# Loading gates late, reordering weights and gathers, and ranking the third batch after the loop, in a fused mLSTM and mixture-of-depths kernel

## The chip, the cores and the metric

The kernel runs on one core of one Trainium2 chip. The metric is device time in microseconds (us) for one execution; lower is better. The core has a matrix engine (PE, with its weight loads shown apart as PEld), a vector engine (DVE), a scalar engine (ACT), a general engine (POOL) and a queue engine (SP) which here only issues transfers. Each engine works through its own instructions strictly in the order of the program; engines wait for each other and for transfers on semaphores.

## The reference

```python
# mLSTM cell: q, k, v, o_gate (4, 8, 768, 40), i_gate, f_gate (4, 8, 768)
for t in range(S):
    m_new = np.maximum(f_gate[:, :, t] + m, i_gate[:, :, t])
    f_stab = np.exp(f_gate[:, :, t] + m - m_new)
    i_stab = np.exp(i_gate[:, :, t] - m_new)
    m = m_new
    C = f_stab * C + i_stab * outer(vt, kt)            # per head, 40 x 40
    n = f_stab * n + i_stab * kt
    h_tilde = C @ qt
    denom = np.maximum(np.abs(n @ qt), 1.0)
    y[:, :, t] = sigmoid(o_gate[:, :, t]) * h_tilde / denom
x = y.transpose(0, 2, 1, 3).reshape(4, 768, 320)
# mixture of depths, capacity 128 of 768 tokens per batch
scores = x @ w_gate
out = x.copy()
for b in range(4):
    top_idx = argpartition(-scores[b], capacity)[:capacity]
    xe = x[b, top_idx]
    ye = np.maximum(xe @ w1, 0) @ w2                   # 320 -> 1024 -> 320
    out[b, top_idx] = xe + sigmoid(scores[b, top_idx])[:, None] * ye
```

## The kernel before, in words

All data is float32. The sequence of each batch is cut into three pieces of 256 tokens, so there are N = 12 steps, three per batch; step n belongs to batch n // 3. The schedule is written out by hand: every call in the loop `for n in range(N)` issues its instructions to the engines at that place, and nothing reorders them.

One step of the recurrence consists of these calls, with their lines in the profile. `scores(n)` (L307) multiplies keys and queries on PE into `pS`; `masked(n)` (L313) applies the causal mask on DVE. `turn(n + 1, "kT")` (L241, copies by ACT at L243) transposes the next keys, `widen(n + 1)` (L225, ACT) spreads the next queries. `update(n + 1)` (L274) makes the next state updates in `pU` from keys and the weighted values `wv`; `states(n + 1)` (L286 to L294) sums them on DVE. `read(n)` (L329) multiplies the queries with the state, `turn(n + 1, "qT")` (L241, copies L245) transposes the next queries, `attend(n)` (L339) adds the part inside the piece, and `divide(n)` (L348 to L353) makes `y` on DVE. `weigh(n)` (L253, POOL) forms `wv` from the loaded values.

A second group of calls turns `y` into output rows: `sigmoid(n)` (L257, ACT) on the loaded gate `o`, `output(n)` (L361, POOL) into the row tile `x`, `router(n)` (L376, DVE) for the scores, `store(n)` (L368, SP) to memory. There are four gate buffers, three buffers each of k, q and v, two row tiles `x` (batches alternate), and four buffers of `y`.

The third group is the mixture of depths for a whole batch. `spread(b, ...)` (L404 PE, L408 ACT) copies the scores of a batch to all partitions; `ranks(b)` counts for each token how many scores are larger, three columns on DVE (`greater`, L414) and three on ACT (`signs`, L419); `select(b)` (L453) makes a selection matrix, `numbers(b)` (L498) turns it into row numbers on PE, `fetch(b)` (L504) gathers the 128 chosen rows from memory by POOL's queue. `fetched(b)` (L514) transposes them, `valued(b)` (L524) computes their gates, `layer1` (L543, L547) and `layer2` (L559) are the two matrix products, `weighed(b)` (L564) scales and `add(b)` (L568) adds the rows to the output with a scattering transfer. The last batch is ranked in two parts (`ranks_first`, `ranks_last`) and its rows are picked by matrix products (`picked`, L479) and not by a gather.

SP issues all loads and stores in one queue: `load(n)` (two transfers each for v and k, one for q), `load_o(n)` (L75, four transfers), `store(n)` (two). `load(n + 3)` stands at the head of step n and carries the gate of step n + 2 with it until step 5; the weights of both layers are issued at the head of step 5 behind step 8's loads. The gates of steps 6 to 8 come with `load(9)`.

In the order before, batch 0 is spread at the end of step 3, ranked in step 5 and its layers stand in step 8; batch 1 is spread at the end of step 6, ranked in step 7, and its layers stand in steps 9 and 10; batch 2 is spread at the end of step 9, ranked and gathered in step 10, and its layers stand in and behind step 11. `fill` calls issue matrix products without use.

## Time and profile before

| | |
|---|---|
| time, median of 4 runs | 168.75 us (167.16 to 170.33) |
| the profiled execution's own time | 169.06 us |
| its span in the profile | 167.3 us |
| granted clock of TensorE, mean | 0.984 |
| PE busy | 147.9 us (88%) |
| PEld, DVE, ACT, POOL busy | 128.1, 95.9, 76.0, 68.3 us |
| transferred | 24.14 MB, mean 144 GB/s |
| read and written in memory | 19.04 MB, 4.59 MB |

The span is what the profile's records cover; 1.76 us of the execution's own time lie around it. PE's busy time counts every matrix product from start to modelled end, so 88% does not mean that the array is used to 88%. The transfers are made of rows of 160 bytes for k, v and o, and of 320 bytes for q; of 94,424 packets 88,465 are smaller than 512 bytes. Start times of instructions below are from the start of the span.

### The profile page before, as it was taken

The page shows a single profiled execution, that of the slowest core. Times are in us where ns is not written, and L with a number is a line of the kernel's source. Part 1 is how long each engine was busy: PE and PEld are TensorE (multiplying, and loading weights), DVE is VectorE, ACT ScalarE, POOL GpSimd, SP SyncE. Part 2 cuts the span into 40 slices and gives each one's busy share as a digit, 9 for nine tenths or more (in the row PEclk, how much of TensorE's full clock was granted, in tenths as well). Part 3 has the DMA queues.
Part 4 walks back from the last instruction along what each step waited for, and adds up shares of the span by engine and source line. Part 5 has one row for each costly group of instructions (what it writes and reads, how often), then busy time and mean ns, then how long its engine had stood idle before and what let it go on. Part 6 is the DMA issues. An engine that isn't in the chain of part 4 may idle for free.

```text
span 167.3 us, 6707 instructions
## 1 busy us (share of the span) xinstructions
PE 147.9 (88%) x2872; PEld 128.1 (77%) x2872; DVE 95.9 (57%) x250; ACT 76.0 (45%) x144; POOL 68.3 (41%) x89
## 2 busy tenths in 40 slices
PE   7979999799989699797999988859999999999930
PEld 7769989697969599696897777639869989799710
DVE  6477466376646998769630039845695796802000
ACT  1567564443645852394321353423934339521110
POOL 7036393928092808162006028942520682230030
PEclk9999999999999999999999999978999999999997
DMA  4999989898898889689969986999778261330003
GB/s 90 195 162 157 155 164 155 160 158 163 139 196 144 152 141 250 114 197 309 318 157 205 214 161 101 171 179 173 136 158 232 62 104 22 80 35 4 8 12 43
DMA packets 94424, 24.14 MB, mean 144 GB/s; under 512 B 88465, under 2 KB 93778, under 8 KB 94386
## 3 DMA queue, kind: packets, MB, share of 16 engines
q1 hardware_dynamic: 93472, 22.36, 70.1%
q0 software_dynamic: 720, 1.15, 4.0%
q8 instruction: 24, 0.39, 1.0%
q10 hardware_dynamic: 194, 0.13, 0.3%
q14 instruction: 14, 0.11, 0.2%
HBM read 19.04 MB, written 4.59 MB: 141 GB/s over the span
## 4 chain that ended last, share of the span: by engine, by line
PE 30%; DMA 30%; SPq 18%; POOL 8%; issue 5%; DVE 3%; ACT 2%; POOLq 1%; ACTq 0%; DVEq 0%
DMA v<-in_v_dram 13%; SPq L64 8%; DMA k<-in_k_dram 7%; SPq L75 6%; POOL wv L253 6%; PE py L559 5%; PE pU L543 5%; PE pt L241 4%; DMA q<-in_q_dram 4%; DMA w<-in_moe_w_dram 4%; PE pU L274 4%; PE pH L339 3%; SPq L68 3%; DMA o<-in_o_gate_dram 2%; PE pH L329 2%
## 5 line engine op out<-in xcount | busy, mean ns | idle before, releaser
L253 POOL TENSOR_TENSOR wv<-v,cols 64x656 f32<-64x656 f32 x23 | 30.6, 1333 | 51.9 <-DMA v<-in_v_dram 43.0
L361 POOL TENSOR_TENSOR x<-y,o 128x320 f32<-128x320 f32 x24 | 21.2, 919 | 10.0 <-DVE x L394 3.8
L243 ACT COPY kT<-pt 128x512 f32<-128x512 f32 x24 | 13.6, 586 | 18.8 <-PE pt L241 18.6
L245 ACT COPY qT<-pt 128x512 f32<-128x512 f32 x24 | 13.8, 634 | 17.1 <-PE pt L241 17.1
L241 PE MATMUL pt<-ident,k 128*128 128x128 f32 x96 | 14.8, 284 | 5.7 <-DMA k<-in_k_dram 5.2
L286 DVE TENSOR_TENSOR C<-pU,C 128x164 f32<-128x164 f32 x40 | 13.1, 328 | 10.7 <-PE pU L274 9.6
L376 DVE CUSTOM_DVE_ANT_0 scr<-x,wg 128x320 f32<-128x320 f32 x22 | 16.1, 730 | 3.8 <-POOL x L361 1.8
L559 PE MATMUL py<-w,hT 128*128 128x320 f32 x64 | 18.2, 437 | 0.0
L274 PE MATMUL pU<-wv,k 128*64 128x82 f32 x384 | 17.1, 245 | 0.5 <-POOL wv L253 0.5
L241 PEld LDWEIGHTS pt<-ident,k 128*128 128x128 f32 x96 | 10.9, 144 | 8.6 <-issue 3.5
L274 PEld LDWEIGHTS pU<-wv,k 128*64 128x64 f32 x384 | 15.1, 143 | 2.6 <-POOL wv L253 1.5
L339 PE MATMUL pH<-wv,P 128*64 128x82 f32 x384 | 16.5, 237 | 0.0
L339 PEld LDWEIGHTS pH<-wv,P 128*64 128x64 f32 x384 | 14.5, 136 | 2.0 <-issue 1.5
L559 PEld LDWEIGHTS py<-w,hT 128*128 128x128 f32 x64 | 11.8, 190 | 4.7
L329 PE MATMUL pH<-C,qT 40*64 40x41 f32 x704 | 14.3, 229 | 0.8 <-issue 0.8
L313 DVE TENSOR_TENSOR P<-pS,mask 128x1024 f32<-128x1024 f32 x12 | 14.6, 1215 | 0.6 <-PE pS L307 0.6
L241 PE MATMUL pt<-ident,qw 128*128 128x128 f32 x96 | 13.1, 279 | 1.9 <-ACT qw L225 1.9
L307 PE MATMUL pS<-qT,kT 40*64 40x64 f32 x768 | 14.3, 221 | 0.3 <-ACT qT L245 0.3
L329 PEld LDWEIGHTS pH<-C,qT 40*64 40x64 f32 x704 | 12.7, 134 | 2.3 <-issue 1.1
L307 PEld LDWEIGHTS pS<-qT,kT 40*64 40x64 f32 x768 | 12.5, 134 | 1.7 <-ACT qT L245 0.5
L568 POOL DMA_INDIRECT out_dram<-yg,idx x4 | 6.4, 1603 | 16.8 <-ACT yg L564 16.3
L419 ACT ACTIVATE sgn<-sb,x 128x768 f32<-128x768 f32 (+2 forms) x16 | 12.8, 801 | 0.4
(138 smaller groups left out, 213.6 us busy)
## 6 DMA issues: line engine op xcount, KB each, us to landing
k<-in_k_dram SPq DMA_DIRECT2D x24, 160.0 KB, 4.6
q<-in_q_dram SPq DMA_DIRECT2D x12, 320.0 KB, 5.4
v<-in_v_dram SPq DMA_DIRECT2D x24, 160.0 KB, 4.3
o<-in_o_gate_dram SPq DMA_DIRECT2D x48, 80.0 KB, 3.7
out_dram<-x SPq DMA_DIRECT2D x24, 160.0 KB, 3.6
w<-in_moe_w_dram SPq DMA_DIRECT2D x2, 640.0 KB, 8.9
w<-in_moe_w_dram SPq DMA_DIRECT2D x2, 512.0 KB, 6.4
w1c<-in_moe_w_dram SPq DMA_DIRECT2D x4, 64.0 KB, 5.3
```

What stands on the lines that cost most here:

```text
L241: PE.transpose(pt[:, p, :], src[:, c, 2 * p:2 * p + 2, :].rearrange("s j d -> s (j d)"), ident)
L243: ACT.copy(out=T[:, :, 128 * c:128 * c + 128], in_=pt)
L245: ACT.copy(out=T.rearrange("e p (u t) -> e t p u", t=2)[:, c], in_=pt)
L253: (DVE if n == 0 and r else POOL).tensor_tensor(out=wv_t[n % 3][o, :, :, r], in0=v_t[n % NB][o], op=OP.mult, in1=cols[s][o, 0:2, b * H:b * ...
L274: PE.matmul(pU[64 * j:64 * j + 64, c, p], k_t[n % NB][:, c, 2 * p + j, :], wv_t[n % 3][:, c, 2 * p + j], start=True, stop=True)
L307: PE.matmul(pS[o, j, c, p, :], kT[e, p, t], qT[e, p, t], start=True, stop=True)
L313: DVE.tensor_tensor(out=P.rearrange(flat), in0=pending[n].pop("pS").rearrange(flat), op=OP.mult, in1=mask.unsqueeze(1).to_broadcast([128, ...
L329: PE.matmul(g["pH"][64 * c:64 * c + 64, NP * j + p, r], g["qT"][e, p, t], state[n, 2 * c + r][e, p, :], start=(c, j) not in g["begun"], st ...
L339: PE.matmul(g["pH"][64 * c:64 * c + 64, NP * j + p], g["P"][:, j, c, p, :], wv_t[n % 3][:, c, 2 * p + j], start=(c, j) not in g["begun"], ...
L361: POOL.tensor_tensor(out=x.rearrange(order, j=2, d=D), in0=pending[n]["y"][:, r].rearrange("s (j p) d -> s j p d", j=2), in1=o.rearrange(o ...
L376: DVE.tensor_tensor_reduce(out=scr, in0=x[:, r, 0:DM], in1=wg, scale=1.0, scalar=0.0, op0=OP.mult, op1=OP.add, accum_out=x[:, r, DM:DM + 1])
L559: PE.matmul(d["py"], d["hT"][:, f, :], w2[:, f, :], start=(f == 0), stop=(f == NF - 1))
```

## The change

Gates: `load` no longer carries the gate of step n + 2. The gates of steps 0 to 3 are issued behind the loads of steps 3, 5, 6 and 7, those of steps 4 and 5 behind the loads of step 9, those of steps 6 to 9 at the head of step 9 behind the stores of steps 3 to 5, and those of steps 10 and 11 behind the whole loop. `opened(n)`, that is `sigmoid` and `output`, moves with them: steps 0 to 5 are opened in steps 3, 4, 5, 7, 8, 8 and steps 6 to 10 behind the loop. There are eight buffers of `y`.

Weights: they are issued in step 6 behind step 8's loads and the stores of steps 0 to 2, and ahead of step 9's loads.

Batches: batch 0 is spread and ranked at the end of step 6, selected and gathered in step 7, with its layers in step 8; batch 1 is ranked at the end of step 9, gathered in step 10, with both layers behind the loop. Batch 2 is ranked in two parts, gathered, and computed behind the loop. Useless products stay in two places only.

```diff
     def load(n):
-        if n < N:
-            load_kv(n, v_t, v)
-            load_kv(n, k_t, k)
-            for i in {8: (2,), 9: (3, 4, 5)}.get(n, ()):
-                store(i)
-            load_q(n)
-            for i in {7: (0, 1)}.get(n, ()):
-                store(i)
-        for i in {7: (), 8: (), 9: (6, 7, 8), 11: (), 12: (10, 11)}.get(n, (n - 1,) if n <= N else ()):
+        load_kv(n, v_t, v)
+        load_kv(n, k_t, k)
+        load_q(n)
+        for i in {3: (0,), 5: (1,), 6: (2,), 7: (3,), 9: (4, 5)}.get(n, ()):
             load_o(i)
...
-            (DVE if n == 0 and r else POOL).tensor_tensor(out=wv_t[n % 3][o, :, :, r], in0=v_t[n % NB][o], op=OP.mult,
+            (DVE if n in (0, 10) and r else POOL).tensor_tensor(out=wv_t[n % 3][o, :, :, r], in0=v_t[n % NB][o], op=OP.mult,
...
+    def opened(n):
+        sigmoid(n)
+        output(n)
...
     for n in range(N):
-        if n > 0:
+        if 0 < n < 9 and n != 6:
             load(n + 3)
-        if n == 5:
-            ...                               # the weights
         scores(n)
+        if n == 10:
+            weigh(11)
         masked(n)
+        if n == 6:
+            for i in range(3):
+                store(i)
+            weights()
+            load(9)
...
+        if n in (7, 10):
+            select(n // 3 - 2)
         if n == 8:
+            fetched(0)
+            valued(0)
             layer1(0, 0)
             layer1(0, 4)
-            layer2(0, 0, 4)
-            layer2(0, 4)
-        if n == 10:
-            layer2(1)
-        if given:
-            ranks(b - 1)
-            select(b - 1)
...
+            layer2(0)
+            weighed(0)
+            weigh(9)
+            opened(4)
+        for i in {4: (0,), 5: (1,), 6: (2,), 8: (3,), 9: (4, 5)}.get(n, ()):
+            router(i)
         if n == 9:
-            fetched(1)
-            ...
-            layer1(1, 0)
-            layer1(1, 4)
+            for i in range(3, 6):
+                store(i)
+            for i in range(6, 10):
+                load_o(i)
         if more:
-            turn(n + 1, "kT", (0, 2, 2, 2, 2, 3, 4, 5)[n] if n < 8 else 0)
+            turn(n + 1, "kT", {6: 2, 9: 4}.get(n, 0))
             widen(n + 1)
         if 0 < n and more:
             update(n + 1)
+            if n == 7:
+                numbers(0, spare(8)[:, 1, 0:3])
+                fetch(0)
             states(n + 1)
         read(n)
         if n == 10:
-            numbers(b - 1, spare(n + 1)[:, 1, 0:3])
-        if n + 2 < N and n != 8:
+            numbers(1, spare(11)[:, 1, 0:3])
+            fetch(1)
+        if n < 7:
             weigh(n + 2)
...
             turn(n + 1, "qT")
-            if b > 0 and s == 0:
-                dep[b - 1] = {"sb": spread(b - 1, 0, 2 * NS)}
...
+        if n in (6, 9):
+            i = n // 3 - 2
+            dep[i] = {"sb": spread(i, 0, 2 * NS)}
+            ranks(i)
         attend(n)
         divide(n)
+        for i in {3: (0,), 4: (1,), 5: (2,), 7: (3,), 8: (5,)}.get(n, ()):
+            opened(i)
         if n == 8:
+            weigh(10)
+            add(0)
...
+    opened(6)
+    opened(7)
+    fetched(1)
+    layer1(1, 0)
+    valued(1)
+    opened(8)
+    for i in range(6, 9):
+        router(i)
+        store(i)
+    load_o(10)
+    load_o(11)
+    dep[2] = {"sb4": spread(2, 0, 4, ps_h)}
+    layer1(1, 4)
+    opened(9)
+    sb = spread(2, 4, 6, ps_h)
+    ranks_first(2)
+    ranks_last(2, sb)
+    select(2)
+    layer2(1, 0, 6)
+    numbers(2, ps_t.tile([128, 3], FP, name="pi", tag="t"))
+    layer2(1, 6)
+    router(9)
+    opened(10)
+    fetch(2)
+    weighed(1)
+    router(10)
+    store(9)
+    store(10)
+    sigmoid(N - 1)
+    gated(N - 1)
+    add(1)
     b = B - 1
+    dep[b] = {"sb4": spread(b, 0, 4)}
+    fetched(2, 2)
+    layer1(2, 0)
+    valued(2)
+    ranks_first(b)
     router_last(N - 1)
     output(N - 1)
     layer1(b - 1, 4)
-    ranks_last(b)
+    ranks_last(b, spread(b, 4, 6))
     store(N - 1)
     layer2(b - 1)
     weighed(b - 1)
     picked(b)
     ...                                       # as before
```

## The prediction

> **What bounds the kernel now.** I read the page first (busy shares, chain), then PE's timeline, the windows of ten microseconds, and the waits. The chain of the page and the longest wait say that transfers and PE share the span:
>
> ```profile
> PE 30%; DMA 30%; SPq 18%; POOL 8%; issue 5%; DVE 3%; ACT 2%; POOLq 1%; ACTq 0%; DVEq 0%
> ...
> POOL wv L253 <- DMA v<-in_v_dram: 43.0, 9, 12.0
> ```
>
> DMA and SP's issuing (SPq) make 48% of the chain, and the weighting of values waits 43.0 us for v. That is the loop. PE's timeline (start, duration, instructions) gives the steps, since each begins with the scores L307, and the end:
>
> ```profile
> 20.32 1.50 PE L307 MATMUL pS<-qT,kT 40*64 40x64 f32 x64
> ...
> 62.77 1.16 PE L307 MATMUL pS<-qT,kT 40*64 40x64 f32 x64
> ...
> 72.44 1.16 PE L307 MATMUL pS<-qT,kT 40*64 40x64 f32 x64
> ...
> 81.48 1.16 PE L307 MATMUL pS<-qT,kT 40*64 40x64 f32 x64
> ...
> 100.30 1.16 PE L307 MATMUL pS<-qT,kT 40*64 40x64 f32 x64
> ...
> 118.64 1.16 PE L307 MATMUL pS<-qT,kT 40*64 40x64 f32 x64
> 119.73 4.57 PE L559 MATMUL py<-w,hT 128*128 128x320 f32 x16
> ...
> 130.50 1.20 PE L307 MATMUL pS<-qT,kT 40*64 40x64 f32 x64
> ...
> 146.23 1.50 PE L479 MATMUL pU<-sel_f,x 128*128 128x128 f32 x12
> ```
>
> I write S6 for the start of step 6 and so on: steps 1, 6, 7, 8, 9, 10, 11 start at 20.3, 62.8, 72.4, 81.5, 100.3, 118.6 and 130.5. The windows (length, then busy time of PE, PEld, DVE, ACT, POOL, then granted clock, DMA share, GB/s) show what limits which part:
>
> ```profile
> 40.00:50.00 10.00, 9.45 (x234) 8.27 (x232) 5.75 (x14) 5.48 (x9) 5.23 (x6) 1.00 0.87 152
> ...
> 110.00:120.00 10.00, 8.58 (x195) 7.79 (x196) 4.49 (x13) 5.12 (x10) 3.86 (x3) 0.83 0.95 160
> ...
> 140.00:150.00 10.00, 10.00 (x70) 8.49 (x69) 5.83 (x22) 5.42 (x16) 3.44 (x3) 1.00 0.22 41
> ```
>
> To 120 us the DMA engines are loaded to 0.8 and more; from 130 us they are nearly free and PE never stops: from S11 to the end, 36.8 us, the kernel is PE's own work without a gap.
>
> **The change, part 1: the loop up to S11.** A step's own products, from start to start, are scores 1.1, keys 1.0, update 1.3, read 1.1, queries 1.0, attend 1.3: 6.8 us. Loads of a step are k, q, v 0.98 MB and the gate 0.33 MB, together 1.31 MB; at the 149 to 170 GB/s of the windows from 10 to 60 us (mean 158) that is 8.3 us, and this is what steps 1 to 8 last now. Without the gate it is 6.2 us, less than PE's 6.8. So steps 1 to 5 become PE's: S6 = 20.3 + 5 x 6.8 = 54.3, 8.5 earlier. The useless products removed (0.28 us each) are hidden now by the wait for loads and are not counted as a gain. Step 6 keeps two (0.55) and has the spread (0.8): S7 = 62.4.
>
> Step 7 has a new wait. The ranks now stand in front of `divide(6)` on DVE and the numbers in the middle of step 7 on PE. The spread ends at 61.2; ACT's copy 0.8, three counts of 1.06 and a correction 0.2, `divide` 1.5, mask 1.2, selection 1.0, numbers 0.3 (rows L408, L414, L426, L348 to L353, L313, L453, L498) end at 69.3. PE finished its update at 65.8 and stands 3.2 us; behind the numbers are read, queries and attend, 3.4: S8 = 72.7. The index takes 0.6 and the gather goes out at 70.0; with the median 4.5 us of the table of issues (3.0 to 6.2) it lands at 74.5, after step 8's scores (73.8). Transposes 0.5, copies 0.8, two halves of layer one at 2.7, layer two 4.5: 85.7.
>
> The transfers by then: up to the queries of step 8, nine loads and four gates and the small gates of the start, 10.4 MB at 158 GB/s from 2 us: 67.6. Stores 0 to 2 and weights, 3.6 MB at the 300 GB/s of the page's slices 19 and 20, take 12 us: 79.6, before layer two needs them. Step 9's load 85.8, gate 4 87.9, gate 5 90, step 10's load 96.2, step 11's 102.4. `opened(4)` puts the sigmoid of gate 4 on ACT ahead of the copies of step 9's keys, which are queued behind it, and PE's queries behind those: 87.9 + sigmoid 0.75 + copies 1.1 + queries widened 0.75 + transposes 1.0 + attend 1.3 gives S9 = 92.8. If the gate is early, yg and PE's own work behind the layers set 91.7; at 149 GB/s the gate lands at 92.3 and S9 is 97.2.
>
> Step 9: scores 1.1, four useless products 1.1, keys, update, read, queries 4.4, spread 0.8, attend 1.3 are 8.7; DVE has divide 1.5, the half of `weigh(10)` 1.66 (row L253 of DVE), mask 1.2 and four routers at 0.58 ahead of the spread, 6.7, as late as PE. S10 = 101.6. Step 10 repeats step 7's wait: from the spread, 1.3 before S10, copy 0.8, counts 3.4, divide 1.5, mask 1.2, selection 1.0, numbers 0.3, then queries and attend 2.3: S11 = S10 + 9.2 = 110.8. That is 19.7 us earlier than 130.5. Ten of it are not gained but carried behind the loop: both layers of batch 1 (5.4 and 4.5).
>
> **Part 2: from S11 to the end.** Times from S11. Read waits for `divide(10)` to 1.5; attend ends at 4.1, `fetched(1)` 4.6, copies 5.5, first half of layer one 8.2, its relu on ACT 8.8. Only then come, in ACT's order, the small gate and the sigmoid of step 8 (9.75); output 1.7 on POOL (11.5), the router's second half (12.4), the second spread 0.5 (12.9). Meanwhile ACT has a copy, a relu and the sigmoid of step 9 and ends the copy of the second spread at 13.9. The ranks of batch 2 follow on ACT, with these rows (four of the first, three of 0.51 with the same 0.19, and gaps):
>
> ```profile
> 138.43 0.71 ACT L419 ACTIVATE sgn<-sb,x 128x512 f32<-128x512 f32 x1
> 139.04 0.19 ACT L419 ACTIVATION_READ_ACCUMULATOR sgn<-sb,x 128x1 f32 x1
> ```
>
> that is 4 x 0.85 + 3 x 0.63 = 5.3: 19.2. DVE joins the counts 0.4, selects 1.0, numbers and index 0.9: 21.6. The gather without traffic beside it takes 3.0:
>
> ```profile
> 131.05 1.05 POOL L504 DMA_INDIRECT xe<-out_dram,idx  x1 [8.86 <-DVE den L349]
> ```
>
> (`fetched(2)` ran at 134.09). It lands at 24.7; the spread of batch 3, two useless products and the transposes end at 25.9, copies 26.8, layer one's first half 29.5. PE, which had layer two of batch 1 in between, stands about 4.4 us (16.3 to 20.7) and again some 2. From there on the order is that of before: its relu started at 137.85 and the first half of the last selection was ready some 7.8 us later, so `picked` starts at 37.5, and from it (146.23) to the end are 21.1 as before. Sum 58.6 against 36.8: 21.8 more.
>
> **Part 3: the clock.** The row of 110 to 120 us shows 0.83: PE stood for 1.0 and 1.7 us around 109 to 111, and keys and update then took 1.09 and 2.23 in place of 0.66 and 1.35 us. That is 10 x 0.17 = 1.7 us for one drop. The hole of 4.4 us behind the loop is longer; I count one drop, 1.7. Bounds: none, 0, if layer one comes after the clock is back; three, 5.1, with those of steps 7 and 10. The Trainium skill, TensorE: Matmul & The Clock Gate, section "What's actually happening", says that the clock falls to half after an idle window of about 3.4 us and comes back after one of work. By that rule only the hole behind the loop counts, 172.9 in all; by this trace, where two holes of 2.7 us together were enough, step 7's would count too. The rule speaks against a change that opens a hole of 4.4 us.
>
> **Sum.** 110.8 + 58.6 + 1.7 = 171.1 of span against 167.3, and 1.76 around it: 172.9 us. The profiled execution took 169.06, 0.2% above the median of 168.75.
>
> **Rivals.** (1) Slower transfers: at 149 GB/s gate 4 is 4.4 later and so is all behind it: 177.3. For it: most windows of the loop lie at 149 to 165. Against: without gates there are fewer, larger transfers in the queue. (2) No difference: the gates come at 170 GB/s (S9 = 91.7) and the clock holds: 109.7 + 58.6 + 1.76 = 170.1, within 1%, which is about what a measurement can tell from no change. (3) Faster: the ranks and the gather of batch 2 run beside PE's work, so that behind S11 only that work counts: 36.8 as now, and layers, transposes, spread and numbers carried there, 12.0: 48.8. Then 110.8 + 48.8 + 1.76 = 161.4; if half of the chain is hidden, 166.3. It decides from the point where step 8's router ends by S11 + 4 and not at 12.4, 8 us earlier. For it: POOL and DVE have idle time in steps 10 and 11, and gates 6 to 9 land by about 114 us. Against: step 8's sigmoid stands behind a relu of layer one on ACT, and the routers stand behind `divide(11)` on DVE. (4) That the gates' removal brings nothing because PE stays behind anyway is excluded for steps 1 to 5: the wait for v is 43 us.
>
> **Chances.** Forecast 0.45; slow transfers 0.18; no difference 0.15; faster 0.22. The forecast's own range is 170 (no gate wait, no drop) to 178 (two more drops, a gather of 6.2). The range reaches down to 165.5, past half of the hidden chain, and up to 178. Faster 0.22, same 0.15, slower 0.63.
>
> **What would show it.** Right: S6 near 54, S7 near 62, a stand of PE of 3 us in step 7 ahead of L494 (the numbers), S9 near 93 with ACT waiting for o ahead of the copies of the keys, S11 near 111, a hole on PE ahead of the numbers of batch 2, and `picked` 37 us behind S11. Wrong: S11 well before 108, or no hole behind the loop, would make it faster; S9 at 97 or more points to the transfers.

## The result, and the profile after

The changed kernel takes 186.03 us (median of 12 runs, 183.03 to 191.0); the kernel before takes 169.06 us beside it (17 runs). The ratio is 1.095, 95% interval 1.090 to 1.100. The profiled execution took 183.03 us with a span of 180.9 us, at a mean granted clock of 0.933 (before: 167.3 us, 0.984). Executions of one kernel spread by a few per cent; ratios are formed without the disturbed ones ("none" stands below where too few were left), and the profiled executions of e2_pick2, e8_step9, e9_early_gather and e10_tail2 are disturbed ones, so that their starts are rather too late and their tails too long.

The profile's chain of work that ended last, shares of the span by engine:

```profile
PE 55%; DVE 12%; DMA 10%; issue 7%; SPq 6%; ACT 3%; POOL 3%; POOLq 0%; DVEq 0%; ACTq 0%
```

Transfers and SP's issuing were 48% of it and are now 16%. What takes their place is PE, DVE and "issue". The waits (total, times, longest) say the same of the values:

```profile
POOL wv L247 <- DMA v<-in_v_dram: 29.7, 7, 6.3
```

PE's timeline (start, duration, instructions, in brackets the idle time before) has the starts of the steps, in the order 1, 6, 7, 8, 9, 10, 11 (the rows of L301 without idle time before them), the idle times that no wait explains ("issue"), and the last selection:

```profile
17.55 1.21 PE L268 MATMUL pU<-wv,k 128*64 128x82 f32 x27 [0.79 <-issue]
...
21.00 1.15 PE L301 MATMUL pS<-qT,kT 40*64 40x64 f32 x61
23.13 0.33 PE L301 MATMUL pS<-qT,kT 40*64 40x64 f32 x3 [0.98 <-issue]
...
40.98 0.31 PE L323 MATMUL pH<-C,qT 40*64 40x41 f32 x2 [0.31 <-issue]
...
57.17 0.93 PE L301 MATMUL pS<-qT,kT 40*64 40x64 f32 x48
59.33 0.46 PE L301 MATMUL pS<-qT,kT 40*64 40x64 f32 x16 [1.23 <-issue]
...
66.55 1.16 PE L301 MATMUL pS<-qT,kT 40*64 40x64 f32 x64
...
73.03 0.31 PE L494 MATMUL pU<-place,sel 128*128 128x3 bf16 x6 [1.82 <-DVE sel L449]
73.27 1.14 PE L323 MATMUL pH<-C,qT 40*64 40x41 f32 x64
74.35 1.60 PE L235 MATMUL pt<-ident,qw 128*128 128x128 f32 x8
75.88 2.45 PE L333 MATMUL pH<-wv,P 128*64 128x82 f32 x32
78.26 1.16 PE L301 MATMUL pS<-qT,kT 40*64 40x64 f32 x64
81.21 0.52 PE L510 MATMUL pX<-ident,xe 128*128 128x128 f32 x3 [1.79 <-DMA xe<-out_dram,idx]
82.19 3.38 PE L539 MATMUL pU<-xeT,w 128*128 128x128 f32 x16 [0.46 <-ACT xeT L512]
...
99.63 1.16 PE L301 MATMUL pS<-qT,kT 40*64 40x64 f32 x64
...
109.86 1.16 PE L301 MATMUL pS<-qT,kT 40*64 40x64 f32 x64
...
117.53 0.29 PE L494 MATMUL pU<-place,sel 128*128 128x3 bf16 x6 [1.73 <-DVE C L280]
...
120.67 1.99 PE L301 MATMUL pS<-qT,kT 40*64 40x64 f32 x64
...
140.67 0.32 PE L494 MATMUL pi<-place,sel 128*128 128x3 bf16 x6 [3.93 <-DVE sel L449]
...
147.50 3.17 PE L539 MATMUL pU<-xeT,w 128*128 128x128 f32 x16 [0.46 <-ACT xeT L512]
...
159.21 1.50 PE L475 MATMUL pU<-sel_f,x 128*128 128x128 f32 x12
```

Set beside before and the forecast (us; "tail" is from S11 to the end of the span):

| | S1 | S6 | S7 | S8 | S9 | S10 | S11 | tail | span |
|---|---|---|---|---|---|---|---|---|---|
| before | 20.3 | 62.8 | 72.4 | 81.5 | 100.3 | 118.6 | 130.5 | 36.8 | 167.3 |
| forecast | 20.3 | 54.3 | 62.4 | 72.7 | 92.8 | 101.6 | 110.8 | 60.3 | 171.1 |
| after | 21.0 | 57.2 | 66.6 | 78.3 | 99.6 | 109.9 | 120.7 | 60.2 | 180.9 |

So the late gates do make steps 1 to 6 faster, by 5.9 us at S7. By S9 the lead is 0.7 us: the wait for the gathered rows and 2.45 us for an `attend` that takes 1.36 at full clock stand in the rows above. At S11 the lead is 9.8 us, and that is no more than batch 1's layers (9.9 us), which before stood in steps 9 and 10 and now stand behind the loop. The tail is 23.4 us longer. The windows (length, busy PE, PEld, DVE, ACT, POOL, clock, DMA share, GB/s):

```profile
40.00:50.00 10.00, 9.69 (x276) 8.72 (x272) 7.07 (x17) 6.13 (x10) 5.99 (x6) 1.00 0.93 153
70.00:80.00 10.00, 7.60 (x206) 6.72 (x204) 5.89 (x16) 3.04 (x5) 2.94 (x3) 0.83 0.92 278
...
110.00:120.00 10.00, 6.94 (x208) 6.38 (x207) 7.77 (x20) 5.82 (x13) 0.77 (x1) 0.96 0.66 107
140.00:150.00 10.00, 8.30 (x33) 5.89 (x34) 6.27 (x23) 2.57 (x7) 7.92 (x8) 0.51 0.48 98
```

Before, the window 140 to 150 had PE busy for 10.00 at full clock. Now it follows the hole of 3.93 us and runs at 0.51. On ACT the ranks of batch 2 that the hole waits for:

```profile
136.71 0.72 ACT L416 ACTIVATE sgn<-sb,x 128x512 f32<-128x512 f32 x1
137.33 0.19 ACT L416 ACTIVATION_READ_ACCUMULATOR sgn<-sb,x 128x1 f32 x1
```

### The profile page after: what moved, and what is told of

Its sections match the earlier page's. It is cut to its first block, busy times and chain, and to the rows that moved or that the text cites. A ratio compares the mean times of both kernels' runs of the same rounds, so it can differ in the third digit from the quotient of the medians.

```text
span 180.9 us, 6677 instructions
## 1 busy us (share of the span) xinstructions
PE 151.8 (84%) x2840; PEld 130.3 (72%) x2840; DVE 96.0 (53%) x259; ACT 76.8 (42%) x153; POOL 67.6 (37%) x88
## 4 chain that ended last, share of the span: by engine, by line
PE 55%; DVE 12%; DMA 10%; issue 7%; SPq 6%; ACT 3%; POOL 3%; POOLq 0%; DVEq 0%; ACTq 0%
PE pt L235 9%; PE pH L333 6%; PE pU L268 6%; PE pU L539 6%; DMA xe<-out_dram,idx 5%; PE pS L301 5%; PE py L555 5%; PE pH L323 4%; SPq L75 3%; PE ph L539 3%; PE warm L102 3%; DVE scr L370 3%; DMA v<-in_v_dram 2%; DVE P L307 2%; DVE cmp L411 2%
## 5 line engine op out<-in xcount | busy, mean ns | idle before, releaser
L247 POOL TENSOR_TENSOR wv<-v,cols 64x656 f32<-64x656 f32 x22 | 29.4, 1338 | 40.8 <-DMA v<-in_v_dram 29.7
L555 PE MATMUL py<-w,hT 128*128 128x320 f32 x64 | 19.5, 457 | 0.0
L333 PE MATMUL pH<-wv,P 128*64 128x82 f32 x384 | 18.5, 252 | 0.4 <-DVE P L307 0.4
L333 PEld LDWEIGHTS pH<-wv,P 128*64 128x64 f32 x384 | 16.1, 148 | 2.7 <-issue 1.6
L301 PE MATMUL pS<-qT,kT 40*64 40x64 f32 x768 | 15.5, 229 | 2.6 <-issue 2.2
L370 DVE CUSTOM_DVE_ANT_0 scr<-x,wg 128x320 f32<-128x320 f32 x22 | 14.6, 664 | 3.7 <-POOL x L355 1.4
L301 PEld LDWEIGHTS pS<-qT,kT 40*64 40x64 f32 x768 | 13.5, 142 | 4.3 <-issue 2.8
L416 ACT ACTIVATE sgn<-sb,x 128x512 f32<-128x512 f32 (+2 forms) x20 | 14.4, 722 | 0.6
L235 PE MATMUL pt<-ident,k 128*128 128x128 f32 x96 | 13.4, 279 | 1.2 <-DMA k<-in_k_dram 1.0
L539 PE MATMUL pU<-xeT,w 128*128 128x128 f32 x80 | 12.6, 323 | 2.1 <-ACT xeT L512 1.4
L539 PEld LDWEIGHTS pU<-xeT,w 128*128 128x128 f32 x80 | 11.8, 234 | 3.3 <-ACT xeT L512 2.4
```

What stands on the lines that cost most here:

```text
L235: PE.transpose(pt[:, p, :], src[:, c, 2 * p:2 * p + 2, :].rearrange("s j d -> s (j d)"), ident)
L247: (DVE if n in (0, 10) and r else POOL).tensor_tensor(out=wv_t[n % 3][o, :, :, r], in0=v_t[n % NB][o], op=OP.mult, in1=cols[s][o, 0:2, b * ...
L301: PE.matmul(pS[o, j, c, p, :], kT[e, p, t], qT[e, p, t], start=True, stop=True)
L333: PE.matmul(g["pH"][64 * c:64 * c + 64, NP * j + p], g["P"][:, j, c, p, :], wv_t[n % 3][:, c, 2 * p + j], start=(c, j) not in g["begun"], ...
L370: DVE.tensor_tensor_reduce(out=scr, in0=x[:, r, 0:DM], in1=wg, scale=1.0, scalar=0.0, op0=OP.mult, op1=OP.add, accum_out=x[:, r, DM:DM + 1])
L416: ACT.activation(out=sgn[:, 0:w], in_=sb, func=AF.Sign, bias=own, scale=-1.0, accum_out=cnt)
```

## The experiments

The first theory after the result: the tail is as forecast; the miss lies in the loop, S11 9.9 us later than forecast, through PE's holes, the chain of batch 0 in steps 6 to 8 and the counts of batch 1 in steps 9 and 10. The rival was that half clock explains most of it. All starts are from the profiled executions:

| kernel | S7 | S8 | S9 | S11 | tail | clock | median us | ratio to before, 95% |
|---|---|---|---|---|---|---|---|---|
| after | 66.6 | 78.3 | 99.6 | 120.7 | 60.2 | 0.933 | 186.0 | 1.095 (1.090 to 1.100) |
| e1_fill | 65.3 | 75.4 | 99.6 | 119.4 | 59.6 | 0.992 | 180.8 | 1.079 (1.062 to 1.097) |
| e2_pick2 | 67.9 | 78.1 | 102.7 | 124.5 | 56.7 | 0.932 | 182.8 | none |
| e3_pick01 | 65.5 | 73.3 | 99.4 | 116.2 | 60.5 | 0.953 | 181.3 | 1.086 (1.073 to 1.098) |
| e4_gates_early | 71.5 | 83.4 | 105.8 | 127.7 | 57.5 | 0.926 | 189.1 | 1.130 (1.112 to 1.149) |
| e5_tail | 65.7 | 77.8 | 99.5 | 125.4 | 57.5 | 0.901 | 186.4 | 1.108 (1.101 to 1.115) |
| e6_nogate | 64.7 | 76.4 | 96.5 | 118.4 | 59.9 | 0.933 | 180.1 | 1.068 (1.059 to 1.076) |
| e7_pick_pool | 65.3 | 75.7 | 99.9 | 116.7 | 61.8 | 0.933 | 179.9 | 1.063 (1.054 to 1.072) |
| e8_step9 | 65.9 | 77.7 | 100.5 | 121.8 | 60.9 | 0.926 | 185.1 | none |
| e9_early_gather | 68.4 | 86.6 | 104.5 | 122.0 | 60.3 | 0.925 | 181.8 | 1.067 (1.053 to 1.082) |
| e10_tail2 | 68.8 | 81.7 | 102.9 | 125.3 | 59.3 | 0.898 | 182.4 | 1.078 (1.067 to 1.089) |
| e11_gather2 | 69.9 | 76.7 | 94.6 | 111.4 | 60.8 | 0.962 | 176.8 | 1.044 (1.032 to 1.056) |
| e12_tail_fill | 66.9 | 77.0 | 100.4 | 120.5 | 56.4 | 0.976 | 177.8 | 1.065 (1.049 to 1.080) |
| e13_both | 77.1 | 83.9 | 104.0 | 124.1 | 56.1 | 0.948 | 182.2 | 1.080 (1.073 to 1.088) |
| e14_chain0 | 76.8 | 83.6 | 103.0 | 124.2 | 61.4 | 0.911 | 187.1 | 1.109 (1.100 to 1.117) |

**e1_fill: useless products in PE's holes.**

```diff
+ fill(..., 6)          # step 7, ahead of numbers(0); 7 ahead of the gathered rows of batch 0
+ fill(..., 5), (..., 6)  # step 10, ahead of read and of numbers(1); 14 and 3 more in the tail
```

> The changed kernel with useless matrix products put into the places where PE stands: 6 ahead of the numbers of batch 0 in step 7, 7 ahead of the transposes of the rows of batch 0 in step 8, 5 ahead of read(10) and 6 ahead of the numbers of batch 1, 14 ahead of the numbers of batch 2, and 5 in place of 2 ahead of the transposes of the rows of batch 2. Theory of the exposed chain (behind the start of step 11 PE waits for the ranks and the gather of batch 2, 13.5 us more than the work carried there): PE waits for the same things, only the slow products behind the holes get their clock back, which is at most 1.7 us each for step 7, step 8, step 10 and the hole behind the loop; 2 to 5 us less than the change, 178 to 182 us, mean clock above 0.96. Rival, the clock (mean 0.933 against 0.984, 9 us of full-speed work over the span): 8 to 9 us less, 175 us. If the products themselves are in the way: no change or slower.

The clock rose to 0.992, but the span fell only from 180.9 to 179.0 us, and S9 did not move. The half clock alone is therefore not the miss: the time, 180.8 us, is the theory's, and the rival's 175 lies below the interval. PE then waited longer for what it had waited for before: 2.77 us instead of 1.79 for the gathered rows of batch 0.

**e2_pick2: counts of batch 2 replaced by a fixed table.**

```diff
- ranks_first(2); ranks_last(2, sb)
+ dep[2]["cnt"] = perm      # numbers and gather ahead of layer2(1)
```

> The changed kernel without the ranking of batch 2: its counts are left out, a fixed table in their place picks 128 rows, and selection, numbers and gather stand right behind the second spread and ahead of layer two of batch 1; the spreads stay. Theory of the exposed chain: the gather of batch 2 goes out as soon as the stores of steps 6 to 8 have landed, at about 136 us in place of 142.3, and layer one of batch 2 starts some 6 us earlier, with a smaller hole on PE; 6 to 9 us less than the change, 175 to 178 us. Rival, the clock: what falls away is only the hole, 2 to 3 us. Rival, late gates: no gain beyond the step 9 routers, under 2 us.

In this trace the tail fell by 3.5 us, against the theory's 6 to 9. The hole ahead of the numbers went from 3.93 to 0.55 us, but a stand of 2.52 us ahead of batch 3's spread came up, for routers whose gates, 10 and 11, are issued only behind store 8. The chain of batch 2 is real, and another wait of nearly its length lies behind it.

**e3_pick01: counts of batches 0 and 1 replaced by the table.**

```diff
- ranks(i)
+ dep[i]["cnt"] = perm
```

> The changed kernel without the counts of batches 0 and 1 (the spreads stay); a fixed table picks their rows. Theory: the counts stand ahead of divide(6) and divide(9) on DVE and hold PE in steps 7 and 10; without them step 8 starts 3 us earlier and the gather of batch 0 goes out as soon as the stores of steps 0 to 2 have landed (75 us, as now), so that step 9 starts at most 1 to 2 us earlier; step 11 starts 2 us earlier against step 10; together 3 to 5 us less than the change, 179 to 181 us. Rival, transfers set step 9: nothing from step 7, 2 us from step 10 at most. Rival, the counts are the main loss of the loop: 8 us or more less.

S7 to S8 fell from 11.7 to 7.8 us and S9 to S11 from 21.0 to 16.8: those are the prices of the counts. But S9 stayed, as the theory had it. PE's timeline of this kernel:

```profile
73.34 1.16 PE L303 MATMUL pS<-qT,kT 40*64 40x64 f32 x64
81.22 0.87 PE L512 MATMUL pX<-ident,xe 128*128 128x128 f32 x3 [6.72 <-DMA xe<-out_dram,idx]
```

The index was ready by 70.6 us, POOL issued the gather at 74.25, and PE stood 6.72 us instead of 1.79.

**e4_gates_early: gates 0 to 5 loaded where they were before (six gate buffers), all else as changed.**

```diff
- 3: (0,), 5: (1,), 6: (2,), 7: (3,), 9: (4, 5)
+ 1: (0,), 3: (2,), 4: (3,), 5: (4,), 6: (5,)    # and gate 1 behind load_q(2)
```

> The changed kernel with the gates of steps 0 to 5 loaded where the kernel before loads them (behind the loads of steps 1 to 6, six gate buffers), and opened where the change opens them. Theory of the exposed chain: steps 1 to 6 go back to 8.5 us each, step 7 starts at about 72, but the transfers ahead of step 9 are the same bytes in all, so that the loss at step 9 is 2 to 5 us; behind the loop nothing changes; 2 to 5 us more than the change, 187 to 190 us. Rival, the late gates are what makes the change slow: 5 us or more less than the change.

S7 came 4.9 us later and the span was 4.3 us longer (185.2). Late gates by themselves help (the ratio to before is 1.130 without them and 1.095 with them); it is what was moved with them that costs.

**e5_tail: batch 2's chain brought forward into steps 9 to 11.**

```diff
+ load_o(6), load_o(7) behind the loads of steps 10 and 11; gates 10 and 11 ahead of stores 6 and 7
+ opened(6) in step 9, opened(7), (8) in step 10; routers 6 to 8, spread, ranks(2), select in 10 and 11
+ numbers(2), fetch(2) between layer1(1) and layer2(1)
```

> The changed kernel with batch 2's chain brought forward and nothing else: gates 6 and 7 are loaded behind the loads of steps 10 and 11, gate 8 ahead of stores 3 to 5, gate 9 behind them, gates 10 and 11 in steps 10 and 11 ahead of stores 6 to 8; the gates of steps 6 to 8 are opened in steps 9 and 10, their routers stand in steps 10 and 11, the counts of batch 2 are made whole in step 11, and its numbers and gather stand between the layers of batch 1. Theory (behind the loop PE waits for batch 2's chain and for gates 10 and 11; of the 60.2 us from S11 to the end only batch 1's layers and numbers, about 12, were carried there): S11 stays within 2 us of 120.7, S11 to the end falls to 36.8 + 12 = 49 to 52, the time to 172 to 176 us. Rival (the work is in all, and moving DVE's and ACT's share of it into the loop only moves the wait): S11 125 or later, S11 to the end 55 to 57, the time 180 to 184. Second rival (the tail waits for bytes: gates 10 and 11): ACT's sigmoids of steps 10 and 11 wait for their gates for over 3 us and the tail stays above 55.

Theory and rival both missed part: the tail was 57.5 and S11 125.4 us. PE's and POOL's timelines of this kernel:

```profile
116.65 2.46 PE L268 MATMUL pU<-wv,k 128*64 128x82 f32 x32 [5.68 <-POOL wv L247]
```

```profile
111.71 1.68 POOL L355 TENSOR_TENSOR x<-y,o 128x320 f32<-128x320 f32 x2 [7.48 <-ACT o L251]
113.36 3.24 POOL L247 TENSOR_TENSOR wv<-v,cols 64x656 f32<-64x656 f32 x2
```

Output 6 stood on POOL ahead of step 11's values, and waited for a sigmoid that ACT ran behind the counts of batch 1; so PE's update waited for POOL. A moved call was paid for by what was queued behind it.

**e6_nogate: gates 0 to 3 not loaded.**

```diff
- {3: (0,), 5: (1,), 6: (2,), 7: (3,), 9: (4, 5)}
+ {9: (4, 5)}               # the four buffers set to zero at the start
```

> The changed kernel without the loads of gates 0 to 3 (ACT sets the four buffers to zero at the start, so the outputs of steps 0 to 3 are halves); every other instruction stays. 1.3 MB less goes through the queue before step 8. Theory (the 4.2 us that S1 to S7 took beyond its sum are holes on PE that end where a 16 KB block of instructions lands, late because the DMA engines are above 90% busy): the holes become shorter than 1.5 us together, S7 62 to 64 us (66.6 with the gates), S8 72 to 75, S9 94 to 97, the time 176 to 180. Rival (PE's supply of instructions is short whatever the queues carry): S7 66 to 67, holes as long as before, time within 2 us of the changed kernel. Second rival (steps 1 to 7 wait for their own loads, and the holes only stand in for that): S7 60 or less.

S9 came at 96.5 us, as the theory said, and the time at the upper end of its bracket; S7 at 64.7 and S8 at 76.4 missed theirs by 0.7 and 1.4 us. PE's holes without any wait became 1.5 us together instead of 3.3 (0.66, 0.16, 0.16, 0.52). That they depend on how full the queue is was not shown by this, since e1_fill, which loads all gates, has only 1.05 us of them up to S7.

**e7_pick_pool: as e3_pick01, stores 0 to 2 issued by POOL behind their outputs.**

```diff
- for i in range(3): store(i)          # SP, step 6
+ if i < 3: store(i, POOL)             # behind opened(i)
```

> The changed kernel with the counts of batches 0 and 1 left out (a fixed table picks the rows, so other rows go through the layers) and stores 0 to 2 issued by POOL right behind their outputs instead of by SP behind the loads of step 8. With the counts alone left out S8 came at 73.3 but S9 stayed at 99.4, since the gather was issued only behind those stores. Theory (the stores' place in SP's queue set S9): gather 0 is issued at 67 to 70 us, lands by 76, S9 comes at 93 to 96 and the time is 173 to 177 us. Rival (the loads of weights or of step 9, or the half clock behind the wait, set S9 anyway): S9 98 to 100, the time 179 to 181.

The theory's numbers fell, the rival's held: S9 99.9 us. The stores no longer held the gather, but the index itself came 2 us later (72.6; PE had waited 1.52 us for step 8's keys), the gather went out at 73.53 and took 7.0 us.

**e8_step9: POOL makes both halves of step 10's values, numbers in a tile of their own.**

```diff
- n in (0, 10) and r        + n == 0 and r
- numbers(i, spare(...))    + numbers(i, ps_t.tile(...))
```

> The changed kernel with two small edits: POOL makes both halves of the weighted values of step 10 again, as it did before, and the numbers of batches 0 and 1 have a tile of their own in place of the spare corner of the update's tile. Theory (S9 to S11 took 21.0 us for a sum of 18.0 because DVE's half stands in front of the routers and runs slowly beside POOL, and because the numbers of batch 1 wait for the states of step 11, which read the same tile): S9 to S11 18.5 to 19.5, the time 1.5 to 2.5 us less than the changed kernel, 181 to 184. Rival (the spread of batch 1 waits for the outputs on POOL, not for DVE): POOL's 1.3 us more make step 9 longer, S9 to S11 21 to 23, the time the same or 1 us more.

S9 to S11 took 21.3 us, as before this edit (21.0), and the time is too uncertain to tell it from the changed kernel's, or the theory from the rival. In this trace PE waits for the other half:

```profile
105.23 1.35 PE L268 MATMUL pU<-wv,k 128*64 128x82 f32 x32 [1.58 <-POOL wv L247]
```

**e9_early_gather: as e7_pick_pool, select, numbers and gather of batch 0 in step 6.**

```diff
- numbers(0, spare(8)...); fetch(0)      # step 7
+ numbers(0, spare(7)...); fetch(0)      # step 6, ahead of weigh(8) on POOL
```

> The kernel of the run before with the fixed table and POOL's stores, in which also the select, the numbers and the gather of batch 0 stand one step earlier, in step 6 behind store 2 (other rows go through the layers, as there). There the index of batch 0 was made at 72.6 us, the gather took 5.9 us beside the weights and landed at 80.5, PE had waited 3.8 us for it, and S9 stayed at 99.9 although the stores were gone from SP's queue. Theory (the gather's lead is one step short: index, issue and landing take 8 us beside the weights and loads, and nothing of step 8 can go ahead of them on PE): with the gather in step 6 it lands by 71, the layers of batch 0 start at 77, S9 comes at 93 to 96, the time is 173 to 177 us. Rival (S9 is set by bytes: weights, the loads of step 9 and gates 4 and 5 have to come through the same full queue): PE waits for the weights or for the values of step 9 instead, S9 98 to 100, the time 178 to 181.

A miss in S9 (104.5) but a useful one. The gather waited on POOL until 71.85 for store 2, and step 8's values stood behind it, so that PE waited 5.86 us and S8 came at 86.6. From S8 to S9, with the rows there in time, it took 17.9 us instead of 21.4.

**e10_tail2: e5_tail with its places mended.**

```diff
- opened(6) in step 9                    + opened(6) behind weigh(11) in step 10
- opened(7) ahead of masked(10)          + opened(7) behind fetch(1)
- opened(8), router 7 in step 10         + opened(8), routers 7, 8 in step 11 behind masked(11)
```

> The kernel with batch 2's chain brought forward, its places mended: gate 6 is opened behind POOL's weighted values of step 11 instead of ahead of them, gate 7 behind the gather of batch 1, gate 8 and routers 7 and 8 in step 11 behind the masked scores. In the first form POOL stood at gate 6 until 110.9 us, so that PE waited 5.7 us for the values of step 11 and S11 came at 125.4, and behind S11 PE waited 2.2 us for the masked scores that stood behind the routers; the tail was 57.5 us. Theory (the exposed chain of batch 2 is what the tail holds beyond the work carried): S11 within 2 us of 120.7, the tail 50 to 54 us, the time 173 to 177. Rival (PE's own work and its half clock fill the tail, the chain's removal brings other waits): S11 120 to 123, the tail 56 to 60, the time 180 to 184.

Median 182.4 us, by the ratios 2.9 us less than the changed kernel: the time and the tail lie in the rival's brackets, S11 (125.3) in neither. The PE timeline of the profiled execution (186.8 us) shows what was left:

```profile
129.88 0.89 PE L401 MATMUL pB<-ident,x 128*128 128x128 f32 x3 [1.63 <-DVE P L307]
...
137.70 3.79 PE L539 MATMUL pU<-xeT,w 128*128 128x128 f32 x16 [1.79 <-ACT xeT L512]
```

A stand of 1.63 us ahead of the spread of batch 2, 1.79 us for ACT's copy of batch 1's rows, and behind them a layer at half clock, 3.79 us for 2.05.

**e11_gather2: gate 2 with gate 1, and the gather behind step 8's values on POOL.**

```diff
- 5: (1,), 6: (2,)     + 5: (1, 2)       # loads; opened and routed one step earlier
- fetch(0) ahead of weigh(8)             + fetch(0) behind weigh(8)
```

> The kernel of the run before (fixed table for batches 0 and 1, POOL's stores 0 to 2, gather of batch 0 in step 6; other rows go through the layers) with two things mended: the gather stands on POOL behind the weighted values of step 8, not ahead of them, and gate 2 is loaded with gate 1 and opened in step 4 instead of step 5. In the run before the gather was issued only at 71.9 us, because store 2 had been issued at 65.5 behind output 2 at 62.9 to 65.2, and the weighted values of step 8 stood behind it until 78.0, so that PE waited 5.9 us and S8 came at 86.6; from S8 to S9 it took 17.9 us, where the changed kernel takes 21.4. Theory (what sets S9 is the chain gate 2, output 2, store 2, gather 0, layers): output 2 is done by 55, the gather issued by 69 to 70 and landed by 75, S8 comes at 74 to 77, S9 18 us later at 92 to 95, the time is 172 to 177 us. Rival (bytes: the weights, step 9's loads and gates 4 and 5 set S9): PE waits for weights, values or keys of steps 8 and 9, S9 at 98 to 100.

S8, S9 and the time came as the theory said (output 2 only at 59.2 us, not 55). PE's timeline and POOL's:

```profile
76.73 1.16 PE L303 MATMUL pS<-qT,kT 40*64 40x64 f32 x64
77.82 0.55 PE L512 MATMUL pX<-ident,xe 128*128 128x128 f32 x3
78.83 2.05 PE L541 MATMUL pU<-xeT,w 128*128 128x128 f32 x16 [0.46 <-ACT xeT L514]
...
94.59 1.16 PE L303 MATMUL pS<-qT,kT 40*64 40x64 f32 x64
...
111.44 1.16 PE L303 MATMUL pS<-qT,kT 40*64 40x64 f32 x64
```

```profile
70.29 1.14 POOL L502 DMA_INDIRECT xe<-out_dram,idx  x1 [0.28 <-DMA q<-in_q_dram]
```

No wait stands ahead of the gathered rows, the layer runs at full clock (2.05 for 3.38), S9 comes at 94.6 and S11 at 111.4: the forecast's 110.8 within 0.6 us, though S7 was 7.5 us later than forecast and the counts of batches 0 and 1 are not in it. The tail, untouched, stays at 60.8.

**e12_tail_fill: e10_tail2 with useless products in the loop's and the tail's holes, the rows of batch 1 copied first.**

```diff
+ fill 6 (step 7), 7 (step 8), 6 and 6 (step 10), 8 ahead of the spread of batch 2
- fetched(1) behind ranks(2)    + fetched(1); fill 4; ranks(2)
```

> The kernel with batch 2's chain brought forward and its places mended, with useless 128x128 products on PE wherever it stood (6 ahead of the numbers in step 7, 7 ahead of the gathered rows of batch 0, 6 and 6 in step 10, 8 ahead of the spread of batch 2, 4 behind the gathered rows of batch 1), and with the gathered rows of batch 1 turned ahead of the counts of batch 2, so that ACT copies them first. There PE ran at half clock from step 10's numbers to 142.6 us and stood 1.8 us for that copy; the tail was 59.3 us, of which 38.9 lie behind the layers' first half of batch 1. Theory (what is left of the tail beyond the work carried is that half clock and those waits): granted clock above 0.97, the tail 51 to 54 us, the time 174 to 178 us. Rival (the clock and the waits are not additive: the useless products delay the work as much as the clock gives): the tail 56 to 59, the time 180 to 183.

The time hit its bracket (177.8 us) and the clock too (0.976); the tail, 56.4, lies in the rival's. With every part of the work in place this form of the change has the lowest median, and it is still 6.5% slower than before; from e1_fill (7.9%) the intervals do not tell it apart.

**e14_chain0 and e13_both: the chain of batch 0 led forward with its counts in place, alone and together with e12_tail_fill.**

```diff
+ gate 2 with gate 1, opened in step 4; stores 0 to 2 by POOL
+ routers 1, 2 behind attend(5); spread behind scores(6); counts and select in step 6
+ numbers(0) behind attend(6); fetch(0) behind weigh(8)
```

> The changed kernel, all its counts in place, with the chain of batch 0 led forward and nothing else: gate 2 loaded with gate 1 and opened in step 4, routers 1 and 2 at the end of step 5, the spread behind the scores of step 6, the counts and the select in step 6, the numbers behind attend(6), the gather on POOL behind the weighted values of step 8, stores 0 to 2 issued by POOL. Theory (S9 was late because gate 2, output 2, store 2, counts and gather stood one step too close to step 8): the gather is issued at 70 to 72 us and lands by 77, S9 comes at 94 to 97 (99.6 in the changed kernel, 94.6 without the counts), S11 at 115 to 118, the tail as in the changed kernel (60), the time 177 to 180 us. Rival (it was the counts' own work on DVE and ACT in steps 6 and 7 that made S9 late, and it stays wherever it stands): S9 at 98 to 100, the time 181 to 184.

> The kernel of the run before this one (chain of batch 0 led forward, all counts in place) with, besides, batch 2's chain brought forward and the useless products of the kernel that took 177.8 us. Theory (the loop's part and the tail's part are separate and add up): S9 94 to 97, S11 115 to 117, the tail 55 to 57, granted clock above 0.97, the time 172 to 175 us: still slower than before, because about 10 us of batch 1's layers stand behind the loop and are not covered there. Rival (what is gained ahead of S9 is lost behind it, since the loads and gates of steps 9 to 11 come no sooner): S9 94 to 97, but S11 119 or later and the time 176 to 178.

For e14_chain0 neither held, and the result was worse than either number. S7 to S9 took 26.2 us instead of 33.1, and PE no longer stood for the gathered rows; but S6 to S7 took 16.1 us instead of 9.4. There PE stood 4.04 us ahead of the spread,

```profile
66.98 1.54 PE L401 MATMUL pB<-ident,x 128*128 128x128 f32 x6 [4.04 <-DVE P L307]
```

because the routers, at the end of step 5, held DVE ahead of the mask of step 6; S7 came at 76.8. Much of this is slow work on DVE while POOL made the values of step 7 (59.43 to 62.08 us), 2.06 us for an instruction that takes 0.33 at its shortest, and 1.57 for 0.49:

```profile
58.87 2.06 DVE L288 TENSOR_TENSOR C<-C,cols 128x164 f32<-128x164 f32 x1
60.85 1.57 DVE L370 CUSTOM_DVE_ANT_0 scr<-x,wg 128x320 f32<-128x320 f32 x1
```

In e13_both S9 was 104.0 with the same stand (3.93 us), and the time, 182.2, lies above both brackets; but the tail was 56.1, as in e12_tail_fill: in these two kernels the tail's part does not depend on the loop's.

## Why the prediction was wrong

The direction was right, the size not: 172.9 forecast, 186.0 measured, outside the range. What follows is the profiled execution, whose span missed by 9.8 us (180.9 for 171.1); it is the fastest of the twelve, and the other 3 us of the median are not explained here. Point by point, by the prediction's own steps.

**Steps 1 to 5 become PE's: right, 2.2 us too small.** A step from start to start is 6.8 us where nothing interrupts it (S4 at 43.53, S5 at 50.32, S6 at 57.17). But S1 to S7 took 45.6 us for 42.1, and S1 came 0.7 late: 4.2 us, of which 3.3 are four holes on PE that no wait explains (0.79, 0.98, 0.31 and 1.23, in the rows above). The kernel before had one (0.82). It stood for its loads often, and the sum had no term for what appears when it no longer does. That is the largest single error, a term put at nothing, and what causes the holes stays open (last section).

**The stand in step 7: right.** From S7 to the index 7.4 us, forecast 7.5; the stand of 3.2 us came in two, 0.97 for keys and 1.82 ahead of the numbers. What followed was not right: queries and attend took 3.9 us from start to start for 2.3, at half clock.

**What sets S9: the step that failed.** The forecast had the rows of batch 0 at 74.5 us, the layers done at 85.7, and gate 4 as the last to come (87.9). None of it happened. The sigmoid of gate 4 shows no wait on ACT's timeline,

```profile
93.44 0.53 ACT L560 ACTIVATE yg<-py,g 128x320 f32<-128x320 f32 x1 [3.96 <-PE py L555]
93.87 0.73 ACT L251 ACTIVATE o<-o 128x640 f32<-128x640 f32 x1
```

though the gate came late as well: its four transfers were issued from 84.94 us on, some 0.7 us apart, and took about 3.5 us each, so that it landed at about 91 (an estimate from these), ahead of the layers all the same. The index and the gather:

```profile
73.77 0.16 DVE L459 SCALAR_TENSOR_TENSOR idx<-pU,off 128x1 int32<-128x1 f32 x1
75.23 1.26 POOL L500 DMA_INDIRECT xe<-out_dram,idx  x1 [6.29 <-DMA w1c<-in_moe_w_dram]
```

The rows came at 81.1: 3.9 us later because the index was (S7's 4.2), 1.3 because POOL issued the gather 1.3 us behind the index and not at once (0.9 in e7_pick_pool, where no store of SP's could hold it), and 1.4 because it took 5.9 us and not the median 4.5. The kernel before had shown that price: its gather of the same batch, beside the weights too, took 6.2 us, the longest of its three. Then the first half of layer one ran at half clock (3.38 us), and the layers ended at 93.2. The forecast's own lower bound, "PE's own work behind the layers", 91.7, with these 7.5 us added is 99.2; 99.6 was measured. So the bound that was called early became the setter, and every later term went into it. Of the 6.8 us by which S9 was late, 4.2 stood at S7 already; the other 2.7 are the half clock in step 7, the stand of 1.79 us for the rows and the half clock behind it.

The runs show more than one chain behind that. Time from S6 to S9: 42.5 us in the changed kernel; 42.6 with the counts left out (e3_pick01); 42.3 with the lead given and the counts in place (e14_chain0, with the new stand of 4.0 us that its routers made); 34.2 with both (e11_gather2, S6 at 60.4). Without the counts, the gather waits for stores, keys and its own transfer instead; of the runs that load every gate only the one with both gone moves S9 forward. Transfers may have a share besides: without gates 0 to 3 (e6_nogate) it is 40.5. What a better placed chain with its counts would give was not measured, so the shares of counts and lead are not separated. In before it is 37.5: there the counts stand in step 5, and the gather goes out 3.6 us behind S7,

```profile
76.04 1.25 POOL L504 DMA_INDIRECT xe<-out_dram,idx  x1 [1.57 <-DVE P L313]
```

where the changed kernel has 8.7 us. The change took that distance away, since gate 2 came later and the counts with it.

**Steps 9 and 10: 3.0 us too small.** Step 9: the first router took 2.00 us beside POOL and held the spread. Step 10: `numbers(1)` waited 1.73 us for the states of step 11, which read the same tile; the sum had the selection as the last to come. e8_step9 shows that curing these two brings another wait; e3_pick01 shows that the counts of batch 1 as a whole cost 4.2 us here.

**From S11 to the end: right, with some luck.** 58.6 and one clock drop, 60.3; measured 60.2. The hole ahead of the numbers of batch 2 is 3.9 us (forecast 4.4), `picked` stands 38.5 us behind S11 (37.5 in the sum, without the drop). The gather took 3.8 us for 3.0, and the second stand of some 2 us became one of 0.5, since PE ran its work at half clock there. And the term is less simple than the forecast had it: with the counts out (e2_pick2) the tail fell by 3.5 us, with the chain brought forward by 1 to 3 (e10_tail2, e5_tail), with useless products besides by 3.8 (e12_tail_fill). The 48.8 us of the rival (3) was reached by none; what holds the last 7 us (56.1 at best) is only partly seen: about 3 us useless products, and routers in front of the spread. It stays open.

**The clock: mechanism right, price not shown.** Two holes of 0.97 and 1.82 us in step 7 were enough for half clock, as the trace of before had said. The rule of the Trainium skill (TensorE: Matmul & The Clock Gate, "What's actually happening"), by which an idle window of 3.4 us is needed, would have had step 7 at full clock; the rows (2.45 us for an `attend` of 1.36) do not agree. The price of 1.7 us was that of a window at 0.83. The window 140 to 150 us ran at 0.51, by the same reckoning 4.9 us; how much of that was hidden behind PE's waits no run separates, but layer one's first half took 3.17 us for 2.05. With all holes filled (e1_fill) the tail fell by 0.6 us and the span by 1.9, which is less than the executions of one kernel differ, and far from the miss.

**The range.** Each rival moved one term. The five errors, 4.2, 1.4, 1.3, 1.4 and 1.6 us, all had one sign and add up to the 9.9 us at S11. A step was costed by its own work, with the last wait named and every other taken as early, so an error could only make it longer.

## What to carry to other kernels

When a change makes a stream-bound loop compute-bound, cost again every chain that used to finish in the slack, from its first input (here the gate) through store, index, issue and gather, with the time that its transfers take beside the others, and ask which two end within a few us of each other: taking one away will then show nothing. A call that is moved forward on an in-order engine is paid for by the next call behind it, so move it only behind the work that the loop waits for. Work carried out of a loop is no gain at the loop's end: subtract it before believing the lead.

## What the runs showed of the hardware

**PE stands at fixed instructions without a wait.** In run after run, the hole in step 6 is at the same place, with 16 products of the scores left, for 1.23 us here and between 0.30 (e13_both) and 1.97 us (e9_early_gather) in all others but e5_tail, which has none there. Up to S7 the DMA view shows an instruction queue that brings a block of 16 KB every 4 to 6 us, and each of the four holes ends 1.3 to 1.8 us after one of its blocks has landed; other blocks land there with no hole behind them. That the supply of instructions causes them is argued from this, not shown by an experiment. Their sum up to S7 varies from 1.05 us (e1_fill) to 3.97 (e9_early_gather) in kernels that load the same bytes until then. The Trainium skill (Runtime: NRT & Kernel Launch, "Instruction fetch mechanics") says that crossing such a block is mostly hidden; whether the 3.3 us of holes here are such crossings no run shows.

**A router takes four times as long beside POOL.** DVE's timeline in step 9, while POOL made step 10's values, and POOL's row:

```profile
104.11 1.85 POOL L247 TENSOR_TENSOR wv<-v,cols 64x656 f32<-64x656 f32 x1
...
104.31 2.00 DVE L370 CUSTOM_DVE_ANT_0 scr<-x,wg 128x320 f32<-128x320 f32 x1
...
106.47 0.49 DVE L370 CUSTOM_DVE_ANT_0 scr<-x,wg 128x320 f32<-128x320 f32 x1
```

The Trainium skill (SBUF — State Buffer, "Who interferes with whom") says that a DVE instruction with two inputs in SBUF contends with a GpSimd instruction that reads it, and that the later one blocks. The rows agree: the router started 0.20 us after POOL's instruction and ended 0.35 us after it, with 0.49 us of work of its own. The slow rows of e14_chain0 above fit less well: the first of them started 0.56 us ahead of POOL's values and was still held.

**A gather of 128 rows takes longer beside weights.** From its issue to the transposes that wait for it 5.7 to 7.1 us in step 8 of the runs in which PE stands for it (in the changed kernel 6.0, with the DMA engines busy to 0.93 from 75.2 to 81.1 us), and 3.8 us behind the loop (issued at 142.31, transposed from 146.13, DMA at 0.55).
